# A three-part kernel on one core: the first layer's sums of results spread over four points, and two attention groups re-timed

## The chip, the cores and the metric

The kernel runs on one core of a Trainium2 chip. The metric is the device time of one launch in microseconds (us). Three runs of the kernel before gave 1128.75, 1129.05 and 1133.09 us, median 1129.05.

## The reference

```python
# chunked attention: 4 x 8 heads, 768 positions, 64 wide, chunks of 32 with 16 left, 8 right, 8 memory rows
scores = scale * np.matmul(q_c, k_full.transpose(0, 1, 3, 2))
scores = scores - np.max(scores, axis=-1, keepdims=True)
a = np.exp(scores); a = a / (np.sum(a, axis=-1, keepdims=True) + 1e-09)
out[:, :, c_start:c_end] = np.matmul(a, v_full)
x = attn_out.transpose(0, 2, 1, 3).reshape(3072, 512)
# layer 1
h = x @ w_in; r = np.maximum(h, 0.0); x = (r * r) @ w_out          # 512 -> 2048 -> 512
# layer 2
h = x @ w_in2; sp = log1p(exp(h)); out = (h * np.tanh(sp)) @ w_out2
```

## The kernel before

The 3072 tokens are three groups of 1024. A layer takes eight steps for each group, and each step handles 256 of the 2048 inner columns. So steps 0 to 7, 8 to 15 and 16 to 23 are the first layer of groups 1, 2 and 3, and steps 24 to 47 the second layer. In a step the kernel multiplies tokens by the first weights in seven block products instead of eight (a Strassen-like scheme, so sums and differences of blocks are needed as operands), applies the activation, and in the next step multiplies by the second weights in eight "units" that are added up in the tiles y0 and y1 (512 columns of 4 x 128 rows each). Each operand is held as a rounded part and a rest, so a product is six matmuls of 128x512.

A step of the first layer is thus 15 stretches of six matmuls. Between them are 15 "points", numbered 0 to 14, where the order written by hand puts everything else. Below, 9.3 is point 3 of step 9. `at(s, i, work)` (L634) plans work for a point, `rest()` (L677) is called once at each point: it first issues the stores that `later()` collected (`flush`, L129), then the loads of weights, then the planned work. The points of a first-layer step follow the products P1, P6, P5, then units 0 and 1, then P2, P7, then units 2, 3, 4, then P4, P3, then units 5, 6, 7. Each engine runs its instructions in the order in which they are written, and all DMAs go out in order on one queue, SP, whose instruction waits until the buffer that it writes or reads is ready; what is behind it waits too.

What is planned beside the products:

- Attention. The tokens' 12 blocks of 256 (p = 0 to 11) are attended four to a group. Group 1's (p 0 to 3) comes before step 0; group 2's (p 4 to 7) is planned in steps 0 to 6, group 3's (p 8 to 11) in steps 9 to 14. `plan_attention` (L638) gives each block's works at fixed distances: scores S at 0, softmax at 1 and 2, exponentials and the next block's k load at 3, normalization and the v load at 5, transposes T at 12, the next q load at 13, values V at 16, copy and block differences (on POOL) at 17 and 18, the store of the result at 22. `start, first, period` (L882) say where the blocks begin and how far apart they are.
- The input of a group, written by those stores, is loaded in the group's last step before (`load_x`, at points 0 to 6 of steps 7, 15 and 23), then rounded on ACT and its rest taken on DVE (`split_x`, L275 and L277).
- The weights are unpacked (DVE L154 to L158) and split (`plan_w`): rounding R, r on ACT, rests L, l on DVE, stores to DRAM (`w_d<-hi`, `w_d<-val`).
- The first layer's result of a group. `sums_y` (L615), called at the end of steps 8, 16 and 24, stores three blocks of y0 and y1 (b11 and b21 are the halves of y0, b12 and b22 those of y1) and computes four differences T1 = b12-b11, T2 = b22-T1, T3 = b22-b12, T4 = b21-T2 on DVE (L628) into fresh tiles, which are stored too.

Buffers have names ("tags"), and a new tile of a tag waits for the users of the old one. The tags of this change: y0 and y1; at0 (k of groups 2 and 3, two x loads, T1 and T2 before); at1 (v and the result `stage` of groups 2 and 3, two x loads, T3 and T4 before); xt0 to xt2 (q, p, transposed p, x loads, a weight's rounded half).

After P6 the DVE adds u1 to the bank of P6 (u2, L744), and P7 reuses that bank; u3 (L763) does the same after P7, c21 is L771, c12 L776. L549 adds a unit to y and frees its bank; in a group's first step ACT copies instead (L547).

Of the kernel before, what the change touches and what calls it, by code (L numbers as in the profile page):

```python
# [53 lines left out]
def tile_chunk_attention_moe_moe2(  # L54
# [470 lines left out]
    def unit(s, t, d, rest):  # L525

        layer, sb, j = where(s)
        ps = bank(3 + units[0] % (3 if sb < NSB - 1 else 5))
        units[0] += 1
        w = w2_t[s].rearrange("p c (b f) -> p c b f", b=4)  # L530

        blk = lambda f: (2 + f, f)[d // 2]
        order = [(f, a, 0) for f in range(2) for a in range(2)] + [(f, 0, 1) for f in range(2)]
        for i, (f, a, c) in enumerate(order):
            nc.tensor.matmul(  # L535
                out=ps,
                lhsT=w[:, a, blk(f), d % 2 * 128:d % 2 * 128 + 128],
                rhs=g_t[s, (f, t)][:, c, :],
                start=i == 0,
                stop=i == len(order) - 1,  # L540
            )
        rest()
        if j == 0 and d == 0:
            y_t[sb, t] = pool.tile([128, KD, NB], FP32, tag=f"y{t}", name="y")
        y = y_t[sb, t][:, d]
        if j == 0:
            nc.scalar.copy(out=y, in_=ps)  # L547
        else:
            nc.vector.tensor_tensor(out=y, in0=ps, in1=y, op=ALU.add)  # L549
# [62 lines left out]
        store_y(sb, i, t, m)  # L612
        flush()

    def sums_y(sb):  # L615
        d = xt_d[1][sb]
        y0, y1 = y_t[sb, 0], y_t[sb, 1]
        b11, b21, b12, b22 = (i.rearrange("p k s -> p (k s)") for i in (y0[:, 0:2], y0[:, 2:4], y1[:, 0:2], y1[:, 2:4]))
        nc.sync.dma_start(out=d[:, B11], in_=b11)
        nc.sync.dma_start(out=d[:, B21], in_=b21)  # L620
        nc.sync.dma_start(out=d[:, B22], in_=b22)
        if sb < NSB - 1:
            both = [pool.tile([128, 2, 2 * NB], FP32, tag=f"at{n}", name="ty") for n in range(2)]
            t = [both[n // 2][:, n % 2] for n in range(4)]
        else:
            t = [pool.tile([128, 2 * NB], FP32, tag=("xt0", "xt1", "xt2", "at1")[n], name="ty") for n in range(4)]
        for n, (t1, t2) in enumerate(((b12, b11), (b22, t[0]), (b22, b12), (b21, t[1]))):
            nc.vector.tensor_tensor(out=t[n], in0=t1, in1=t2, op=ALU.subtract)  # L628
            later(d[:, T1 + n], t[n])


    beside = {}

# [4 lines left out]
    def plan_attention(s, i, p):  # L638

        for n, work in {  # L640
# [1 line left out]
            1: lambda: softmax(p, 0),  # L642
            2: lambda: softmax(p, 1),
            3: lambda: (exps(p, 0), exps(p, 1), load_k(p + 1) if (p + 1) % PSB else None),
            5: lambda: (normalize(p), load_v(p) if p > PSB else None),
            12: lambda: transpose_p(p),
            13: lambda: (copy_pt(p), load_q(p + 1) if (p + 1) % PSB else None),
            16: lambda: values(p),
# [2 lines left out]
            22: lambda: store_x(p),  # L651
        }.items():
            at(s, i + n, work)

    def plan_w(s, i, e, order, round_, split, val):

# [15 lines left out]
    def step(s):  # L672
# [113 lines left out]
            for w in beside.pop((s, i), []):  # L786
                w()
        flush()
        if prev and where(s - 1)[0] == 0 and where(s - 1)[2] == NQ - 1:
            sums_y(where(s - 1)[1])  # L790

    with tc.manual_schedule():
        nc.scalar.preload_act_table_set("natural_log_exp_and_others")
# [74 lines left out]
        seconds = [e for e in order_w if e[0]]  # L868
        for n, e in enumerate(seconds):
            if n < NQ - 1:  # L870
                plan_w(NQ + n, 0, e, "Aa|D|d|RS|s|L||||r|l", lambda e, i: round_w2(e, i, "xt2"), split_w2, "val")
            else:
                n -= NQ - 1
                hi = (["xt0", "xt1"], ["xt2", "at1"])[n % 2]
# [4 lines left out]

        for sb in range(NSB - 1):  # L880
            p = PSB * (sb + 1)
            start, first, period = ((0, 4, 25), (NQ + 1, 8, 19))[sb]  # L882
            at(start, 0, lambda p=p: load_q(p))
            if sb:
                at(start, 0, lambda p=p: load_k(p))
            for n in range(PSB):
                plan_attention(start, first + period * n, p + n)

        for sb in range(1, 2 * NSB):
            s = sb * NQ - 1  # L890
# [80 lines left out]
```

## Time and profile before

| | us |
|---|---|
| median of three runs | 1129.05 |
| the profiled execution, its own time | 1126.08 |
| its span (first to last instruction) | 1124.2 |
| TensorE (PE) busy in the span | 1061.5 |
| VectorE (DVE) busy | 898.6 |
| ScalarE (ACT) busy | 561.6 |
| GpSimd (POOL) busy | 430.5 |

The span is the time from the first to the last instruction of the profiled execution; its own time is 1.9 us longer. A time in a row is counted from the span's start. L480 is a product with the first weights, L535 a unit, L346 and L354 scores, L416 values. The step that begins at a given time can be told from the L480 row of 18 matmuls (P1, P6, P5) that opens it: steps 7, 8, 9 and 10 begin at 239.34, 264.87, 288.82 and 324.82 us.

How to read the rows further down: in "busy time by stretch" stand the stretch, its length, then busy us and (number of instructions) of PE, PE's weight loads, DVE, ACT and POOL, then the granted clock of PE as a share of its full 2.4 GHz, the busy share of the DMA engines and GB/s. In a "timeline" stand start, length, engine, line, operation, out<-in, shapes and count of instructions merged, and in brackets the idle time before them and what ended it. SPq is an instruction that issues a DMA; its length is the time that issuing took.

### The profile page before, as it was taken

To read this page: it belongs to the slowest core of one execution; us is meant where nothing else is said; L and a number is where in the kernel's file an instruction comes from. 1 tells how busy PE (TensorE), PEld (TensorE's weight loads), DVE (VectorE), ACT (ScalarE), POOL (GpSimd) and SP (SyncE) were. 2 spreads that over 40 slices of the span, in tenths; PEclk is the share of its full clock that TensorE was granted. 3 is DMA by queue.
4 is the path that set the end of the run, shared out by engine and by line. 5 is a ranking of instruction groups with operands and counts; after the bars stand their busy time and mean duration, and the time that the engine had idled before them with its cause. 6 is when DMAs were issued, how large, how long until landed. Compare 5 with 4: busy or idle time off the path is not lost.

```text
span 1124.2 us, 19766 instructions
## 1 busy us (share of the span) xinstructions
PE 1061.5 (94%) x7478; PEld 872.3 (78%) x7478; DVE 898.6 (80%) x1170; ACT 561.6 (50%) x879; POOL 430.5 (38%) x327
## 2 busy tenths in 40 slices
PE   5779999897799999999999999999999999999997
PEld 5758787785677887888888878888878888778885
DVE  5686889969756766578999767988888888978888
ACT  2458555546544554647656555443354444444331
POOL 1215233232223333223322244546454554545552
PEclk9998999999989999999999999999999999999999
DMA  9556867777989898969999968989979889797441
GB/s 354 216 186 269 308 228 275 259 265 268 369 316 319 306 333 298 336 237 381 374 345 328 361 225 292 316 312 324 401 247 319 308 307 371 272 315 227 158 155 75
DMA packets 192125, 324.94 MB, mean 289 GB/s; under 512 B 13344, under 2 KB 151072, under 8 KB 188192
## 3 DMA queue, kind: packets, MB, share of 16 engines
q1 hardware_dynamic: 192032, 323.69, 80.9%
q8 instruction: 60, 0.98, 0.3%
q14 instruction: 33, 0.27, 0.1%
HBM read 231.62 MB, written 92.01 MB: 288 GB/s over the span
## 4 chain that ended last, share of the span: by engine, by line
PE 65%; DVE 14%; DMA 6%; issue 4%; ACT 3%; POOL 1%; SPq 0%; DVEq 0%; ACTq 0%; POOLq 0%
PE banks L480 29%; PE banks L535 16%; PE banks L570 15%; DVE m L558 3%; PE banks L416 1%; PE banks L346 1%; DVE r L521 1%; DMA w_d<-hi 1%; DMA w2s<-w_d 1%; DVE y L549 1%; DMA w1s<-w_d 1%; DVE ty L628 1%; DVE val L157 1%; DVE val L158 1%; DVE val L154 1%
## 5 line engine op out<-in xcount | busy, mean ns | idle before, releaser
L480 PE MATMUL banks<-x,w1s 128*128 128x512 f32 x2016 | 502.2, 396 | 19.1 <-DVE u L763 7.3
L494 POOL TENSOR_TENSOR g<-r,g 128x512 fp32r<-128x512 f32 x206 | 289.6, 1412 | 523.1 <-ACT g L493 434.6
L480 PEld LDWEIGHTS banks<-x,w1s 128*128 128x128 f32 x2016 | 382.3, 191 | 104.4 <-DVE u L763 9.0
L535 PE MATMUL banks<-g,w2s 128*128 128x512 f32 x1152 | 279.7, 394 | 6.9 <-DVE y L549 6.7
L535 PEld LDWEIGHTS banks<-g,w2s 128*128 128x128 f32 x1152 | 216.7, 190 | 55.7 <-DVE y L549 8.4
L570 PE MATMUL banks<-g,w2s 128*128 128x512 f32 x966 | 239.0, 390 | 1.2 <-DVE m L558 0.6
L570 PEld LDWEIGHTS banks<-g,w2s 128*128 128x128 f32 x966 | 180.6, 188 | 41.9 <-DVE m L558 2.3
L558 DVE TENSOR_TENSOR m<-banks,m 128x1024 f32<-128x1024 f32 x144 | 173.3, 1218 | 30.5 <-PE banks L570 27.5
L493 ACT CAST g<-r 128x512 fp32r<-128x512 f32 x206 | 127.0, 621 | 31.0 <-DVE r L521 23.7
L549 DVE TENSOR_TENSOR y<-banks,y 128x512 f32<-128x512 f32 x168 | 111.4, 682 | 25.7 <-PE banks L535 25.4
L494 POOL TENSOR_TENSOR g<-more,g 128x512 fp32r<-128x512 f32 x55 | 81.8, 1492 | 77.8 <-ACT g L493 63.2
L499 ACT ACTIVATE r<-r 128x512 f32<-128x512 f32 x72 | 45.4, 631 | 69.5 <-DVE r L771 46.1
L503 ACT ACTIVATE r<-r 128x512 f32<-128x512 f32 x48 | 30.3, 632 | 75.8 <-DVE r L765 38.4
L213 ACT CAST hi<-val 128x1024 fp32r<-128x1024 f32 (+1 forms) x32 | 30.4, 951 | 71.4 <-DVE val L158 42.3
L500 ACT ACTIVATE r<-r 128x512 f32<-128x512 f32 x96 | 60.7, 633 | 3.1
L154 DVE TENSOR_SCALAR val<-val 128x512 f32<-128x512 f32 x64 | 36.7, 573 | 24.4 <-ACT val L147 24.4
L346 PE MATMUL banks<-k,q 64*32 64x64 f32 x1536 | 39.4, 255 | 16.8 <-DMA k<-k_dram 10.1
L346 PEld LDWEIGHTS banks<-k,q 64*32 64x32 f32 x1536 | 33.4, 125 | 21.5 <-issue 18.2
L158 DVE SCALAR_TENSOR_TENSOR val<-raw,val 128x512 uint32<-128x512 uint32 x64 | 47.3, 738 | 2.2
L735 ACT COPY u<-banks 128x512 f32<-128x512 f32 x48 | 27.9, 581 | 41.1 <-PE banks L480 41.0
L386 POOL TENSOR_TENSOR p<-p,sum 128x512 f32<-128x512 f32 x22 | 25.6, 1186 | 57.8 <-DVE sum L383 23.3
L416 PE MATMUL banks<-pt,v 64*64 64x32 f32 x1536 | 35.1, 249 | 11.3 <-ACT pt L404 9.8
(72 smaller groups left out, 991.4 us busy)
## 6 DMA issues: line engine op xcount, KB each, us to landing
w1s<-w_d SPq DMA_DIRECT2D x280, 256.0 KB, 5.5
w2s<-w_d SPq DMA_DIRECT2D x229, 256.0 KB, 5.4
raw<-w_dram SPq DMA_DIRECT2D x64, 512.0 KB, 5.1
w_d<-w1s SPq DMA_DIRECT2D x8, 1792.0 KB, 7.1
x<-xs_d SPq DMA_DIRECT2D x14, 1024.0 KB, 10.7
k<-k_dram SPq DMA_DIRECT2D x24, 512.0 KB, 7.3
v<-v_dram SPq DMA_DIRECT2D x24, 512.0 KB, 8.7
xt<-xt_d SPq DMA_DIRECT2D x21, 512.0 KB, 7.3
```

The source lines that it names most:

```text
L154: nc.vector.tensor_scalar(out=val, in0=val, scalar1=LIMIT, scalar2=-LIMIT * NEGATIVE, op0=ALU.min, op1=ALU.max)
L158: nc.vector.scalar_tensor_tensor(out=vb, in0=low, scalar=29, in1=vb, op0=ALU.logical_shift_right, op1=ALU.bitwise_or)
L346: nc.tensor.matmul(out=s4[32 * c:32 * c + 32, j, hp, :], lhsT=q_t[p][r0:r0 + 64, j, hp, 32 * c:32 * c + 32], rhs=k_t[p][r0:r0 + 64, j, hp, ...
L416: nc.tensor.matmul(out=x_ps[par][64 * h2:64 * h2 + 64, o:o + 32], lhsT=v_t[p][j][r0:r0 + 64, h2, a, c, :], rhs=pt_t[p][r0:r0 + 64, h2, j, ...
L480: nc.tensor.matmul(out=ps, lhsT=w[:, a, f:f + 128], rhs=x[:, xi, c, kk, :], start=start and i == 0, stop=stop and i == len(order) - 1, ski ...
L493: nc.scalar.copy(out=g[:, 0], in_=r)
L494: nc.gpsimd.tensor_tensor(out=g[:, 1], in0=r, in1=g[:, 0].bitcast(FP32), op=ALU.subtract)
L500: nc.scalar.activation(out=r, in_=r, func=ACTF.Square)
L535: nc.tensor.matmul(out=ps, lhsT=w[:, a, blk(f), d % 2 * 128:d % 2 * 128 + 128], rhs=g_t[s, (f, t)][:, c, :], start=i == 0, stop=i == len(o ...
L549: nc.vector.tensor_tensor(out=y, in0=ps, in1=y, op=ALU.add)
L558: engine.tensor_tensor(out=to, in0=in0, in1=in1, op=ALU.add)
L570: nc.tensor.matmul(out=bank(first + d), lhsT=w[:, a, 128 * d:128 * d + 128], rhs=g[:, c, :], start=i == 0, stop=i == 2)
```

## The change

The four differences are planned at points instead of after a step: T1 at point 13 of the group's last unit step (8.13, 16.13, 24.13), T2, T4 and T3 at points 0, 1 and 3 of the next. T1 and T2 go into one tile of tag at1; T4 and T3 overwrite b21 and b12 in y0 and y1, so the tag at0 is not used any more, and the next group keeps the same y tiles. The stores of b11 and b21 are planned at points 5 and 9. Group 3's attention begins at 8.10 (before 9.8) with 20 points from block to block (before 19); its k is loaded at 8.1 (before 9.0). Group 2's has 24 points from block to block (before 25). The v load comes 8 points after the scores instead of 5. In steps 8 to 14 the second half of a weight is rounded and split a point later.

```diff
@@ unit
-            y_t[sb, t] = pool.tile([128, KD, NB], FP32, tag=f"y{t}", name="y")
+            y_t[sb, t] = y_t[sb - 1, t] if sb else pool.tile([128, KD, NB], FP32, tag=f"y{t}", name="y")
@@
-    def sums_y(sb):
-        d = xt_d[1][sb]
...
-        nc.sync.dma_start(out=d[:, B11], in_=b11)
-        nc.sync.dma_start(out=d[:, B21], in_=b21)
-        nc.sync.dma_start(out=d[:, B22], in_=b22)
-        if sb < NSB - 1:
-            both = [pool.tile([128, 2, 2 * NB], FP32, tag=f"at{n}", name="ty") for n in range(2)]
...
-        for n, (t1, t2) in enumerate(((b12, b11), (b22, t[0]), (b22, b12), (b21, t[1]))):
-            nc.vector.tensor_tensor(out=t[n], in0=t1, in1=t2, op=ALU.subtract)
-            later(d[:, T1 + n], t[n])
@@ plan_attention
-            5: lambda: (normalize(p), load_v(p) if p > PSB else None),
+            5: lambda: normalize(p),
+            8: lambda: load_v(p) if p > PSB else None,
@@
+    def plan_sums(sb):
...
+        def minus(n, to, in0, in1):
+            nc.vector.tensor_tensor(out=to, in0=in0, in1=in1, op=ALU.subtract)
+            later(d[:, n], to)
+        def first():
+            b11, _, b12, _ = blocks()
+            t["both"] = pool.tile([128, 2, 2 * NB], FP32, tag="at1", name="ty")
+            minus(T1, t["both"][:, 0], b12, b11)
+        def second():
+            b22 = blocks()[3]
+            later(d[:, B22], b22)
+            minus(T2, t["both"][:, 1], b22, t["both"][:, 0])
+        def fourth():
+            b21 = blocks()[1]
+            minus(T4, b21, b21, t["both"][:, 1])
+        def third():
+            _, _, b12, b22 = blocks()
+            minus(T3, b12, b22, b12)
+        s = (sb + 1) * NQ
+        at(s, 5, lambda: later(d[:, B11], blocks()[0]))
+        at(s, 9, lambda: later(d[:, B21], blocks()[1]))
+        at(s, 13, first)
+        at(s + 1, 0, second)
+        at(s + 1, 1, fourth)
+        at(s + 1, 3, third)
@@ step
-        if prev and where(s - 1)[0] == 0 and where(s - 1)[2] == NQ - 1:
-            sums_y(where(s - 1)[1])
@@
-                plan_w(NQ + n, 0, e, "Aa|D|d|RS|s|L||||r|l", lambda e, i: round_w2(e, i, "xt2"), split_w2, "val")
+                plan_w(NQ + n, 0, e, "Aa|D|d|RS|s|L|||||r|l", lambda e, i: round_w2(e, i, "xt2"), split_w2, "val")
@@
-            start, first, period = ((0, 4, 25), (NQ + 1, 8, 19))[sb]
+            start, first, period = ((0, 4, 24), (NQ, 10, 20))[sb]
             at(start, 0, lambda p=p: load_q(p))
             if sb:
-                at(start, 0, lambda p=p: load_k(p))
+                at(start, 1, lambda p=p: load_k(p))
             for n in range(PSB):
                 plan_attention(start, first + period * n, p + n)
+        for sb in range(NSB):
+            plan_sums(sb)
```

On DVE, from the end of step 8 into step 9, the kernel before has c12, the last three units, the four differences in a row, one weight half unpacked and then u2:

```order
L776 TENSOR_TENSOR r<-banks,u_2918 128x512
L549 TENSOR_TENSOR y<-banks,y 128x512 x3
L628 TENSOR_TENSOR ty<-y 128x1024
L628 TENSOR_TENSOR ty<-y,ty 128x1024
L628 TENSOR_TENSOR ty<-y 128x1024
L628 TENSOR_TENSOR ty<-y,ty 128x1024
L154 TENSOR_SCALAR val<-val 128x512
L157 TENSOR_SCALAR val<-val 128x512
L158 SCALAR_TENSOR_TENSOR val<-raw,val 128x512
L744 TENSOR_TENSOR u_3107<-banks,u_3093 128x512
```

The same place after the change, from unit 5 on (L651 is a difference, L380 to L383 the normalization of p 8, L769 is u2):

```order
L549 TENSOR_TENSOR y<-banks,y 128x512
L651 TENSOR_TENSOR ty<-y 128x1024
L549 TENSOR_TENSOR y<-banks,y 128x512 x2
L380 TENSOR_REDUCE sum<-p 128x8 x2
L382 TENSOR_SCALAR sum<-sum 128x16
L383 RECIPROCAL sum<-sum 128x16
L651 TENSOR_TENSOR ty<-y,ty 128x1024
L154 TENSOR_SCALAR val<-val 128x512
L157 TENSOR_SCALAR val<-val 128x512
L158 SCALAR_TENSOR_TENSOR val<-raw,val 128x512
L651 TENSOR_TENSOR y<-y,ty 128x1024
L769 TENSOR_TENSOR u_3194<-banks,u_3177 128x512
```

T1 stands among the last units, T2 and T4 are still ahead of u2, and T3 has moved behind it; p 8's normalization is new in this place.

On the SP queue the kernel before issues, at the end of step 8 and the begin of step 9, the stores of the result and only behind them group 3's first q and k:

```order
L619 DMA xt_d<-y 128x1024
L620 DMA xt_d<-y 128x1024
L621 DMA xt_d<-y 128x1024
L131 DMA xt_d<-ty 128x1024 x4
L247 DMA w1s<-w_d 128x2x256
L313 DMA q<-q_dram 128x1024
L318 DMA k<-k_dram 128x1024 x2
L247 DMA w2s<-w_d 128x2x256
```

After the change the queue has, from 8.13 to 9.4 (the first row is p 9's k; p 8's has gone out at 8.1):

```order
L318 DMA k<-k_dram 128x1024 x2
L131 DMA xt_d<-ty 128x1024
L247 DMA w1s<-w_d 128x2x256
L131 DMA xt_d<-y 128x1024
L131 DMA xt_d<-ty 128x1024
L247 DMA w2s<-w_d 128x2x256
L131 DMA raw<-w_dram 128x1024
L131 DMA xt_d<-y 128x1024
L247 DMA w1s<-w_d 128x2x256
L131 DMA raw<-w_dram 128x1024
L331 DMA v<-v_dram 128x1024 x2
L131 DMA xt_d<-y 128x1024
```

The loads of p 8's v, which take the tile of T1 and T2, stand ahead of the store of T3, the last row.

On the same queue the last block of group 2 is stored at the end of step 6. The kernel before:

```order
L131 DMA raw<-w_dram 128x1024 x4
L131 DMA w_d<-w1s 128x3584
L442 DMA xt_d<-stage 128x1792
L131 DMA w_d<-w2s 128x2048
L247 DMA w1s<-w_d 128x2x256
L261 DMA xt<-xt_d 128x4x256 x2
```

The kernel after:

```order
L131 DMA raw<-w_dram 128x1024 x3
L442 DMA xt_d<-stage 128x1792
L131 DMA raw<-w_dram 128x1024
L131 DMA w_d<-w1s 128x3584
L131 DMA w_d<-w2s 128x2048
L247 DMA w1s<-w_d 128x2x256
L261 DMA xt<-xt_d 128x4x256 x2
```

The store has moved past a raw load and a weight store, away from the loads of x that read what it writes.

## Rows read from the trace of the kernel before

**Rows 1.** Busy time by stretch, steps 7 to 10 and step 17.

```profile
239.34:264.87 25.53, 21.59 (x91) 16.59 (x90) 16.38 (x23) 12.61 (x19) 5.58 (x4) 1.00 1.03 377
264.87:288.82 23.95, 21.50 (x92) 16.54 (x90) 19.47 (x30) 13.64 (x20) 5.80 (x4) 1.00 0.72 236
288.82:324.82 36.00, 28.06 (x235) 22.41 (x234) 23.41 (x34) 17.76 (x30) 6.79 (x5) 0.86 1.02 379
324.82:354.23 29.41, 28.23 (x371) 23.36 (x370) 17.49 (x28) 16.63 (x28) 11.38 (x11) 0.94 0.84 289
494.12:514.52 20.40, 20.40 (x91) 16.89 (x90) 16.92 (x27) 12.04 (x21) 3.75 (x4) 1.00 0.94 329
```

**Rows 2.** Timeline of PE, steps 8 and 9.

```profile
270.25 2.98 PE L535 MATMUL banks<-g,w2s 128*128 128x512 f32 x12 [1.13 <-DVE y L549]
...
276.21 1.64 PE L480 MATMUL banks<-x,w1s 128*128 128x512 f32 x6 [1.16 <-DVE u L744]
...
300.26 1.67 PE L480 MATMUL banks<-x,w1s 128*128 128x512 f32 x6 [3.12 <-DVE u L744]
...
307.35 0.65 PE L346 MATMUL banks<-k,q 64*32 64x64 f32 x32 [2.56 <-DMA k<-k_dram]
308.55 0.37 PE L346 MATMUL banks<-k,q 64*32 64x64 f32 x11 [0.54 <-DMA k<-k_dram]
...
313.83 0.31 PE L346 MATMUL banks<-k,q 64*32 64x64 f32 x1 [1.72 <-issue]
```

**Rows 3.** Timeline of SP, begin of step 9.

```profile
293.59 4.83 SPq L131 DMA_DIRECT2D xt_d<-ty  x4
...
300.50 0.88 SPq L318 DMA_DIRECT2D k<-k_dram  x2
```

**Rows 4.** Busy time by stretch, two stretches of lower granted clock.

```profile
308.84:319.06 10.22, 8.50 (x119) 7.11 (x108) 3.64 (x5) 1.63 (x2) 0.20 (x1) 0.50 1.04 380
349.80:353.20 3.40, 3.40 (x10) 2.71 (x9) 1.12 (x2) 1.06 (x2) 1.57 (x2) 0.50 0.72 236
```

**Rows 5.** Timeline of PE, step 7.

```profile
254.51 3.02 PE L480 MATMUL banks<-x,w1s 128*128 128x512 f32 x12 [1.40 <-DVE u L763]
259.04 1.65 PE L535 MATMUL banks<-g,w2s 128*128 128x512 f32 x6 [1.51 <-DVE y L549]
261.65 3.39 PE L535 MATMUL banks<-g,w2s 128*128 128x512 f32 x12 [0.96 <-DVE y L549]
```

**Rows 6.** Timeline of ACT, step 7.

```profile
251.54 1.05 ACT L275 CAST x<-xt 128x1024 fp32r<-128x1024 f32 x1 [8.54 <-DMA xt<-xt_d]
```

**Rows 7.** Chain that ended last, end of step 6: start, us, what.

```profile
237.51 0.71 POOL stage L438
...
238.24 8.18 DMA xt_d<-stage
```

**Rows 8.** Timeline of DVE, begin of step 9.

```profile
291.38 2.19 DVE L628 TENSOR_TENSOR ty<-y 128x1024 f32<-128x1024 f32 x1
...
295.73 1.21 DVE L628 TENSOR_TENSOR ty<-y 128x1024 f32<-128x1024 f32 x1
...
299.52 0.68 DVE L744 TENSOR_TENSOR u<-banks,u 128x512 f32<-128x512 f32 x1
```

**Rows 9.** Groups of instructions of the whole span: busy us, mean ns | idle before.

```profile
L369 DVE TENSOR_REDUCE mx<-banks 128x8 f32<-128x512 f32 x24 | 16.4, 684 | 28.2 <-PE banks L346 17.7 <-PE banks L354 10.6
L380 DVE TENSOR_REDUCE sum<-p 128x8 f32<-128x512 f32 x24 | 15.5, 679 | 1.6 <-ACT p L376 1.4
```

**Rows 10.** Timeline of PE, step 13.

```profile
412.62 0.81 PE L346 MATMUL banks<-k,q 64*32 64x64 f32 x43 [0.99 <-ACT stage L428]
```

**Rows 11.** DMA issues by line: KB each, median us from issue to landing.

```profile
v<-v_dram SPq DMA_DIRECT2D x24, 512.0 KB, 8.7
...
xt_d<-ty SPq DMA_DIRECT2D x12, 512.0 KB, 3.1
```

**Rows 12.** Timeline of POOL, begin of step 9.

```profile
291.19 1.29 POOL L494 TENSOR_TENSOR g<-r,g 128x512 fp32r<-128x512 f32 x1 [5.18 <-ACT g L493]
```

More of the change, by code (lines that the diff above doesn't have):

```diff
@@ L613, in last_unit @@
         flush()
-    def sums_y(sb):
-        d = xt_d[1][sb]
-        y0, y1 = y_t[sb, 0], y_t[sb, 1]
-        b11, b21, b12, b22 = (i.rearrange("p k s -> p (k s)") for i in (y0[:, 0:2], y0[:, 2:4], y1[:, 0:2], y1[:, 2:4]))
-        nc.sync.dma_start(out=d[:, B11], in_=b11)
-        nc.sync.dma_start(out=d[:, B21], in_=b21)
-        nc.sync.dma_start(out=d[:, B22], in_=b22)
-        if sb < NSB - 1:
-            both = [pool.tile([128, 2, 2 * NB], FP32, tag=f"at{n}", name="ty") for n in range(2)]
-            t = [both[n // 2][:, n % 2] for n in range(4)]
-        else:
-            t = [pool.tile([128, 2 * NB], FP32, tag=("xt0", "xt1", "xt2", "at1")[n], name="ty") for n in range(4)]
-        for n, (t1, t2) in enumerate(((b12, b11), (b22, t[0]), (b22, b12), (b21, t[1]))):
-            nc.vector.tensor_tensor(out=t[n], in0=t1, in1=t2, op=ALU.subtract)
-            later(d[:, T1 + n], t[n])
     beside = {}
@@ L653, in plan_attention, with blocks @@
             at(s, i + n, work)
+    def plan_sums(sb):
+        d = xt_d[1][sb]
+        t = {}
+        def blocks():
+            y0, y1 = y_t[sb, 0], y_t[sb, 1]
+            return [i.rearrange("p k s -> p (k s)") for i in (y0[:, 0:2], y0[:, 2:4], y1[:, 0:2], y1[:, 2:4])]
+        def minus(n, to, in0, in1):
[22 more added lines that the diff above has]
+        at(s + 1, 3, third)
     def plan_w(s, i, e, order, round_, split, val):
```

## The prediction

> **What bounds the kernel now.** The times by stretch come first: PE is busy through nearly every step, so a step's length beside that of an undisturbed one says what may be had. Step 17 has neither attention nor idle PE: 90 matmuls in 20.40 us, or 1.36 us for each of its 15 points. Steps 7 to 10 take 25.53, 23.95, 36.00 and 29.41 us [rows 1]; step 9 stands out, with 7.94 us of idle PE (36.00 less 28.06) and a granted clock of 0.86. The timeline of PE says what ends the idle times there. In step 9 PE waits 3.12 us for u2 on DVE, then 2.56 and 0.54 us for k of p 8, then 1.72 us for nothing that the profile shows ("issue") [rows 2]. The wait for u2: the four differences stand in a row ahead of it on DVE, from 291.38 on, and u2 starts at 299.52 [rows 8]. The wait for k: the loads leave SP at 300.50, behind the four stores of the differences, whose issue takes from 293.59 to 298.42 because each waits for its difference [rows 3]; k also takes the tile of T1 and T2. Behind that, 10.22 us stand at a granted clock of 0.50, which is 1.2 GHz, after a stretch of idle PE and score products; a second one, of 3.40 us, follows p 9's scores [rows 4]. Step 7 has another cause: ACT stands 8.54 us until the first x block has landed [rows 6], because its source, the last store of group 2, left at 238.24 as soon as POOL had the differences and took 8.18 us [rows 7]. DVE is late behind ACT, and PE waits 1.40, 1.51 and 0.96 us in step 7 [rows 5], then 1.13 and 1.16 us in step 8 [rows 2].
>
> **The change, term by term.** Attention's own work on PE is the same in all (a block's products move from one step to another), so I count waits and clock only, against the profiled execution's 1126.08 us.
>
> k of p 8. It leaves at 8.1, some 10 points before the scores at 8.10, about 14 us at 1.36. Before, the same loads needed 8 us (300.50 to the end of the wait at 308.55 [rows 2, 3]). At 8.1 its tile at0 must be free of the fourth x block of step 7, whose rest comes on DVE at 7.12; a delay there of a few us is covered. So the 2.56 and 0.54 us go: -3.10. If k is late after all, 0. The "issue" wait of 1.72 us sits inside the scores and no engine ends it: it moves with them, 0.
>
> Clock. In the 10.22 us at 0.50 PE is busy 8.50 us [rows 4]; at full speed that work would take 4.25 us, so it costs at most 4.25. Score products are small and gain less than dense ones: I take -3.5 with the wait ahead of it gone, between 0 and -4.25. The 3.40 us after p 9's scores cost at most 1.70; their place moves from 10.12 to 10.0, where the same drop may come or not: -0.85, the middle.
>
> Step 7. With a period of 24, p 7's values come three points earlier (6.2 for 6.5), so its differences on POOL and its store should be ready about 3 x 1.36 = 4.1 us earlier; and on SP the store has moved past a raw load and a weight store. It would land about 242.3 for 246.4, and ACT's wait of 8.54 us falls to about 4.4, nearer to the point (7.4, about 245 to 246) where ACT would not have done the rounding sooner anyway. The three waits of PE in step 7 are the tail of that delay and sum to 3.87, less than the 4.1 gained: -3.87, between 0 (if POOL or SP is late for another reason) and that. Of step 8's 1.13 + 1.16 = 2.29 the same backlog is a part; I take -1.3, between +1.7 and -2.29: step 8 gets p 8's softmax as new work on DVE, two reductions of 0.68 us [rows 9] and two subtractions of the same size, plus T1 of 1.21 to 2.19 [rows 8]. That makes 19.47 + 2.7 + 1.7 = 23.9 us of DVE for a PE step of 20.40 plus the scores, near 22.4; the excess of 1.5 to 1.7 is what is late next if it is not taken up by step 7's slack (DVE 16.38 of 25.53 us [rows 1]).
>
> u2 in step 9. Ahead of it T1 is gone to step 8 and T3 has moved behind: two of four differences, 3.3 us of the 6.6 between 291.38 and 298.0. New ahead of it are p 8's two sums of normalization, 2 x 0.68 [rows 9], and a small rest, together 1.8. So of 3.12 some 1.6 stay: -1.5, between 0 and -3.12.
>
> The bank for scores. In step 13 p 11's scores wait 0.99 us for ACT to have copied p 10's values out of the bank [rows 10]. Period 20 gives the copy a point more: -0.5, between 0 and -0.99.
>
> What is added. T4 and T3 lie in y0 and y1, and group 2's first units are copied there by ACT (9.7 on for b21, 9.9 on for b12), which must wait until the stores have landed. T2's store goes at 9.1, and p 8's v, which takes the tile of T1 and T2, is loaded at 9.3: SP waits there for the landing, and T3's store stands behind v. A store of a difference takes 3.1 us in the median, of all 12 [rows 11]; beside heavy traffic the store of a block took 8.18 [rows 7]. v then has until 9.11, eight points or 10.9 us, and needs 8.7 [rows 11]: with 3.1 it is in time, with 8.18 late by about 3. Behind ACT's wait at 9.9 stand the rounding of a weight half and the gates of c21 and c12, whose results are needed four points into step 10, so a few us are covered. I take +1.5 for both, nearer to the quiet end because two points lie between T2 and v, and keep 0 to +6. In steps 17 and 25 there is no v behind the differences; 0.
>
> In steps 1 to 6 the two points' shift leaves each block's work in its step; 0, with a bound of 3.5 both ways, one stretch at the lower clock more or less [rows 4].
>
> Sum: -3.10 - 3.5 - 0.85 - 3.87 - 1.3 - 1.5 - 0.5 + 1.5 = -13.1, so 1113.0 for an execution like the profiled one. The runs' median, 1129.05, is 3.0 above that execution's time; the forecast for a median is 1129.05 - 13.1 = 1116.
>
> One rule weighs against the change. T1 took 2.19 us beside POOL, which worked from 291.19 on [rows 12], and T3 of the same shape 1.21 without it [rows 8]. The Trainium skill ("SBUF", Who interferes with whom) says that a DVE instruction with two SBUF inputs contends with a GpSimd instruction that reads SBUF, and that the one that comes second waits for the whole of the first; the two rows agree. At 9.0 POOL gets p 8's normalization in addition, beside T2 and T4; by the rule both take 2.19, 1 us more in all than the mean used above, and the sum is -12.1.
>
> **The rivals.**
>
> DVE is the bound of step 8. For it: 19.47 us of 23.95 busy already, and about 4.4 added. Against it: DVE is idle for 9.15 of step 7's 25.53 us, and without ACT's wait it can start step 8 without a backlog. Then step 8 keeps its 2.29 (the 1.3 taken is lost) and grows by 1.7, and u2 keeps its 3.12 (1.5 lost): 4.5 less than forecast, 1120.5.
>
> The clock takes it back. For it: both stretches at 0.50 follow score products with a wait among them [rows 2, 4], and every scores, transposes and values of eight blocks changes place. Against it: group 3's four blocks have twelve such places, and two of them show a drop. Three new stretches of the price of the larger one, 3.5 each, are 10.5 us: 1126, no change.
>
> The change does not do what it says, k still late: 3.10 + 3.5 come back, 1123.
>
> Slower: the differences in place hold up the queue. SP goes in order: T2 waits for DVE, v for T2's landing, T3's store for v's issue, group 2's copies of b12 for T3. If DVE is 4.5 us late (the first rival) and each transfer takes 8 to 9 us, v lands 4.5 + 8.18 + 8.7 = 21.4 us after T2's point and is due after some 11 points, 15 us, so that PE stands 6.4 us at 9.11 and gets the lower clock (3.5); T3's store follows v and lands as late as v, five points after ACT should have copied b12, so that the bank is missing to unit 7: up to 6.8. With the DVE's 4.5 that is 6.4 + 3.5 + 6.8 + 4.5 = 21.2, 8 more than the gain: 1137 at its worst; from 13.1 on it decides against the change. Against it: 3.1 us for such a store in the median.
>
> **How the numbers follow.** The forecast with its own range, 1109 to 1119, gets 0.58; DVE as the bound of step 8, 0.20; clock, 0.11; k late, 0.04; slower, 0.07. All terms at their full size would be 3.10 + 4.25 + 1.70 + 3.87 + 2.29 + 3.12 + 0.99 = 19.3, and with 3.5 from steps 1 to 6 22.8: 1106, the low end. The high end is the clock's, 1126. A measurement of this kernel can tell about 0.5%, 5.6 us, from no change. Faster by more, under 1123.4: the forecast, the first rival and half of the third, 0.80; within 0.5%: the clock and the rest of k late, 0.13; slower: 0.07.
>
> **What would show it.** Right: in step 9 no wait for k in the timeline of PE, a wait before P7 of about 1.6 us, a granted clock of 1.00 in steps 8 and 9; in step 7 ACT's wait for x at about half and PE's three waits gone; step 9 at about 25 us. Wrong: a wait before p 8's values for v, ACT waiting for a store of y in steps 9, 17 or 25, step 8 above 25 us, or new stretches at 0.50 in steps 1 to 14.

## The result, and the profile after

The changed kernel takes 1115.71 us, the median of four runs (1112.70 to 1119.03); the kernel before took 1128.9 beside it. The ratio is 0.9877 with an interval of 0.9839 to 0.9915, so it is faster, by 13 us. The profiled execution took 1115.43 us (span 1113.6; before 1126.08 and 1124.2). The two profiles thus differ by 10.6 us, less than the medians do: single executions of one kernel lie some us apart, and so each reading below of a few tenths on a whole step is one execution's.

Where the 10.6 us are, by places in the program (from the first matmul of the first step named to the first behind the last):

| place | before | after | difference | forecast there |
|---|---|---|---|---|
| up to step 1 | 78.76 | 77.53 | -1.23 | 0 |
| steps 1 to 6 | 160.58 | 158.01 | -2.57 | 0 |
| step 7 | 25.53 | 24.48 | -1.05 | -3.87 |
| steps 8 to 14 | 188.06 | 182.74 | -5.32 | -9.25 |
| steps 15 to 23 | 184.44 | 184.55 | +0.11 | 0 |
| steps 24 and 25 | 41.15 | 39.44 | -1.71 | 0 |
| behind step 25 | 445.68 | 446.85 | +1.17 | 0 |

The total came out as forecast, the places did not: the steps that the prediction worked on (7 to 14) gave 6.4 of the 13.1 us. The first and the last row are scatter: up to step 1 the thirteen kernels profiled (these two and the eleven of the experiments) take 77.5 to 78.9 us, behind step 25 from 445.7 to 448.4, whatever was changed.

Busy time by stretch of the kernel after: steps 7 to 10 (the first four rows answer to [rows 1]), steps 8 to 14, and steps 24 and 25:

```profile
235.54:260.02 24.48, 21.59 (x92) 16.58 (x90) 16.47 (x23) 12.70 (x19) 5.60 (x4) 1.00 1.02 378
260.02:286.96 26.94, 24.45 (x236) 19.03 (x234) 22.45 (x35) 16.18 (x25) 7.03 (x5) 1.00 0.89 311
286.96:315.06 28.10, 25.23 (x227) 20.55 (x226) 19.16 (x29) 14.11 (x25) 7.82 (x5) 0.94 1.02 379
315.06:341.99 26.93, 24.57 (x243) 20.10 (x242) 17.95 (x32) 15.37 (x26) 10.23 (x11) 1.00 0.87 319
260.02:442.76 182.74, 171.83 (x1736) 139.86 (x1734) 129.59 (x208) 95.24 (x155) 61.28 (x52) 0.98 0.89 316
627.31:666.75 39.44, 39.44 (x175) 32.67 (x174) 28.77 (x33) 23.57 (x34) 17.50 (x12) 1.00 0.83 273
```

The same for the kernel before, steps 8 to 14, and steps 24 and 25:

```profile
264.87:452.93 188.06, 174.25 (x1735) 142.25 (x1734) 131.12 (x211) 98.97 (x160) 60.92 (x53) 0.96 0.89 313
637.37:678.52 41.15, 40.03 (x176) 32.51 (x174) 28.25 (x33) 23.33 (x34) 17.17 (x12) 1.00 0.75 260
```

Single steps can't be set side by side, because score products have moved (step 8 has x236 matmuls for x92, step 9 x227 for x235); the seven together can, with x1736 and x1735. Idle PE in them fell from 13.81 to 10.91 us (length less the first number behind it), busy PE by 2.42. With the same number of products it is the clock that makes busy time differ: at 0.50 stood 10.22 + 3.40 us before [rows 4], and 3.41 + 3.41 after:

```profile
297.70:301.11 3.41, 2.96 (x7) 2.39 (x8) 3.31 (x7) 1.46 (x3) 0.00 (x0) 0.50 0.98 331
383.03:386.44 3.41, 3.41 (x32) 2.77 (x25) 1.23 (x2) 2.04 (x5) 1.31 (x2) 0.50 0.97 312
```

The timeline of PE after, steps 7 to 10, waits only (start, length, instruction, wait ahead of it and what ended it), answers to [rows 2, 5]:

```profile
249.65 3.02 PE L480 MATMUL banks<-x,w1s 128*128 128x512 f32 x12 [0.35 <-DVE u L788]
254.18 1.66 PE L535 MATMUL banks<-g,w2s 128*128 128x512 f32 x6 [1.52 <-DVE y L549]
256.79 3.39 PE L535 MATMUL banks<-g,w2s 128*128 128x512 f32 x12 [0.95 <-DVE y L549]
...
265.39 3.00 PE L535 MATMUL banks<-g,w2s 128*128 128x512 f32 x12 [1.13 <-DVE y L549]
...
271.41 1.64 PE L480 MATMUL banks<-x,w1s 128*128 128x512 f32 x6 [1.21 <-DVE u L769]
...
298.15 2.93 PE L480 MATMUL banks<-x,w1s 128*128 128x512 f32 x6 [2.87 <-DVE u L769]
...
318.16 0.33 PE L346 MATMUL banks<-k,q 64*32 64x64 f32 x8 [1.58 <-ACT stage L428]
```

The two waits for k and the "issue" wait of step 9 are gone; the waits of step 8 stand as they were; u2's is 2.87 for 3.12; and p 9's scores in step 10 have a new one of 1.58.

### The profile page after: what moved, and what is told of

It reads as the page before. It is cut to its first block, busy times and chain, and to the rows that moved or that the text cites. A ratio compares the mean times of both kernels' runs of the same rounds, so it can differ in the third digit from the quotient of the medians.

```text
span 1113.6 us, 19772 instructions
## 1 busy us (share of the span) xinstructions
PE 1056.0 (95%) x7478; PEld 867.1 (78%) x7478; DVE 903.5 (81%) x1170; ACT 561.1 (50%) x879; POOL 432.8 (39%) x327
## 4 chain that ended last, share of the span: by engine, by line
PE 59%; DVE 9%; DMA 3%; issue 2%; ACT 1%; SPq 0%; DVEq 0%; ACTq 0%
PE banks L480 28%; PE banks L570 17%; PE banks L535 13%; DVE m L558 3%; DMA w_d<-hi 2%; DMA w_d<-val 1%; DVE r L521 1%; DVE more L521 0%; DVE y L549 0%; DVE u L769 0%; DVE val L220 0%; PE banks L346 0%; PE banks L416 0%; DVE val L157 0%; DVE val L154 0%
## 5 line engine op out<-in xcount | busy, mean ns | idle before, releaser
L213 ACT CAST hi<-val 128x1024 fp32r<-128x1024 f32 (+1 forms) x32 | 30.4, 950 | 76.0 <-DVE val L158 43.5
L154 DVE TENSOR_SCALAR val<-val 128x512 f32<-128x512 f32 x64 | 41.1, 642 | 29.8 <-ACT val L147 29.8
L220 DVE TENSOR_TENSOR val<-val,hi 128x1024 f32<-128x1024 f32 (+1 forms) x32 | 36.3, 1136 | 19.3 <-ACT hi L213 19.0
L158 DVE SCALAR_TENSOR_TENSOR val<-raw,val 128x512 uint32<-128x512 uint32 x64 | 48.1, 751 | 2.2
L386 POOL TENSOR_TENSOR p<-p,sum 128x512 f32<-128x512 f32 x22 | 27.1, 1251 | 52.6 <-DVE sum L383 25.5
L147 ACT ACTIVATE val<-raw 128x512 f32<-128x512 f32 x64 | 40.2, 664 | 11.9 <-DMA w_d<-val 11.8
```

Source lines behind the costliest of these rows:

```text
L147: nc.scalar.activation(out=val, in_=high.bitcast(FP32), func=ACTF.Prelu, scale=REBIAS, alpha=NEGATIVE)
L154: nc.vector.tensor_scalar(out=val, in0=val, scalar1=LIMIT, scalar2=-LIMIT * NEGATIVE, op0=ALU.min, op1=ALU.max)
L158: nc.vector.scalar_tensor_tensor(out=vb, in0=low, scalar=29, in1=vb, op0=ALU.logical_shift_right, op1=ALU.bitwise_or)
```

## Experiments

The theory: the time comes from k behind the differences and from the lower clock that followed that wait, so the four points alone should bring most of it. The rivals: the shorter period of group 2, the early start of group 3, or the places of v and of the weight half carry it. Ratios are to the kernel before, with 95% intervals; lengths are of one profiled execution each.

**The differences at four points, alone.** The kernel before, with the shared tiles of y and `plan_sums` as in the change, all else old:

```diff
-        if prev and where(s - 1)[0] == 0 and where(s - 1)[2] == NQ - 1:
-            sums_y(where(s - 1)[1])
+        for sb in range(NSB):
+            plan_sums(sb)
```

> Theory A (k's loads stood behind the differences' stores and took their tile): the differences at four points alone take k out of that queue, so the wait for k in step 9 (3.10 us) goes with the lower clock behind it, step 25 keeps the gain of the spread differences, 1120 to 1123 beside 1129. Rival B (the gain is the 13 points by which group 3's attention begins earlier): with the blocks in their old places little is gained, 1126 to 1128, and step 9 stays above 32 us.

Measured: 1124.27 us, 0.9963 (0.9944 to 0.9983). No wait for k is left, yet steps 8 to 14 take 190.11 us, 2 more than before. The timeline of PE in this kernel, steps 9, 10 and 13, shows what stands there instead:

```profile
297.85 1.66 PE L480 MATMUL banks<-x,w1s 128*128 128x512 f32 x6 [1.33 <-ACT u L759]
...
309.20 0.31 PE L346 MATMUL banks<-k,q 64*32 64x64 f32 x1 [1.96 <-issue]
...
342.18 0.32 PE L346 MATMUL banks<-k,q 64*32 64x64 f32 x8 [1.33 <-ACT r L499]
347.80 0.80 PE L346 MATMUL banks<-k,q 64*32 64x64 f32 x18 [3.18 <-issue]
...
414.01 0.81 PE L346 MATMUL banks<-k,q 64*32 64x64 f32 x43 [2.35 <-ACT stage L428]
```

And its stretches of lower clock there, by busy time:

```profile
346.68:353.50 6.82, 5.70 (x30) 4.47 (x30) 2.67 (x4) 1.85 (x3) 2.23 (x3) 0.50 0.79 283
414.95:421.77 6.82, 6.82 (x104) 5.88 (x96) 3.23 (x5) 1.25 (x2) 4.31 (x5) 0.50 0.92 309
309.13:312.54 3.41, 3.34 (x10) 2.59 (x11) 0.69 (x1) 0.63 (x2) 0.99 (x1) 0.50 1.04 397
```

Step 9 falls from 36.00 to 29.72 us; steps 10 and 13 give it back (34.40 and 31.43 us, for 29.41 and 26.57 before). So the wait was rightly named, but all that the four points change, steps 24 and 25 included, is worth about 4 us (0.0037 of 1127): 17.05 us stand at 0.50 in steps 8 to 14 for 13.62 before, in other places, behind other waits in or ahead of scores. The theory holds for the wait and falls for the time (1120 to 1123).

**Group 3's early start undone.** The changed kernel with the old start, first point and period of group 3:

```diff
-            start, first, period = ((0, 4, 24), (NQ, 10, 20))[sb]
+            start, first, period = ((0, 4, 24), (NQ + 1, 8, 19))[sb]
```

> The kernel after with group 3's blocks back at 9.8, period 19. Theory A: no wait for k either, within 3 us of the kernel after (1113 to 1119). Rival B: it loses most of the gain, 1122 to 1127.

Measured: 1115.49 us, 0.9893 (0.9866 to 0.9920), against 0.9877 of the change: the early start isn't what brings the gain. Step 9 then waits in its scores, 2.83 us of "issue", but step 10 has no wait for the stage copy. The thirteen profiles of this document agree on that trade. In steps 8 to 14 the seven kernels with the old start, the one before among them, have "issue" waits of PE of 2.7 to 5.1 us in sum and wait 0.6 to 2.4 us for the stage copy in step 13; the six with the early start have no "issue" wait there, and five of them wait 0.8 to 2.7 us for the stage copy in step 10.

**Group 2's period undone, and alone.** The changed kernel with period 25, and the kernel before with period 24:

```diff
-            start, first, period = ((0, 4, 24), (NQ, 10, 20))[sb]
+            start, first, period = ((0, 4, 25), (NQ, 10, 20))[sb]
```

> The kernel after with group 2's period back at 25. Forecast's step: p 7's store leaves later, step 7 takes 1 us more (24.5 to 25.5) and steps 1 to 6 some 2.5 us more: 1118 to 1120. Rival: the period decides nothing that can be measured, 1114 to 1117, and steps 1 to 6 differ by where the lower clock falls.

```diff
-            start, first, period = ((0, 4, 25), (NQ + 1, 8, 19))[sb]
+            start, first, period = ((0, 4, 24), (NQ + 1, 8, 19))[sb]
```

> The kernel before with group 2's period 24 and nothing else. Theory A after the first four runs: the period is worth 3 to 5 us in steps 1 to 7, because the stretches at granted clock 0.50 near 83 and 138 us shorten (together 13.7 us before) and p 7's store leaves earlier; 1123 to 1126 with steps 1 to 6 at 158 us for 160.6. Rival: these stretches fall by chance; 1127 to 1130 and 160 to 161 us.

Measured: 1118.28 us, 0.9906 (0.9876 to 0.9936) without it; 1127.06, 0.9985 (0.9971 to 0.9998) with nothing else. The first is 3.3 us above the change (0.0029 of 1127), with intervals that overlap; the second is 1.7 us below the kernel before, barely clear of noise, and its time lies in the range of the rival, though its steps 1 to 6 fit the theory. So the period is worth some 2 to 3 us, not surely. Steps 1 to 6 by busy time, of the kernel without it and of the change beside it:

```profile
78.23:238.79 160.56, 150.51 (x1501) 123.69 (x1500) 137.19 (x216) 96.15 (x155) 59.65 (x49) 0.96 0.71 257
```

```profile
77.53:235.54 158.01, 146.26 (x1502) 119.45 (x1500) 138.66 (x216) 95.64 (x155) 59.61 (x49) 0.99 0.72 263
```

And of the kernel with the period alone:

```profile
77.77:236.63 158.86, 149.47 (x1502) 122.15 (x1500) 137.88 (x215) 96.37 (x156) 59.81 (x49) 0.97 0.72 263
```

All four profiled kernels with period 25 take 160.25 to 160.76 us for steps 1 to 6; of the nine with 24, eight take 155.3 to 159.4 and one 160.5. But these times go with the time at 0.50 in these steps. All four kernels with period 25 have 13.65 us there (two stretches of 6.83, from 82.98 and 137.60 on in the first row); so have three of the nine with 24, and they take 158.9 to 160.5 us. The one with 10.24 takes 158.9, the three with 3.41 take 157.4 to 158.2, the two with none 155.3 and 156.7. Between the first two rows PE is busy for 4.25 us less with period 24 and idle for 1.70 us more. So the gain in steps 1 to 6, forecast at nothing, is in these profiles that of the clock; that the shorter period makes its low stretches rarer is likely, not shown; at the same 13.65 us the three with period 24 lie 0.1 to 1.6 us below the mean of the four with 25. In step 7 the period shows in every profile: 25.5 to 26.3 us with period 25, 24.5 to 24.9 with 24 (without the early loads further down).

The kernel with the period alone shows one thing more. Its k loads still stand behind the four stores (they leave SP at 297.05), and yet PE does not wait for k: a stretch at 0.50 from 296.13 on slows the products ahead (twelve of a unit take 4.51 us, before 3.02), and the scores begin only at 303.98. The timeline of PE in step 9 has this wait instead:

```profile
310.15 0.26 PE L346 MATMUL banks<-k,q 64*32 64x64 f32 x1 [3.61 <-issue]
```

Step 9 takes 36.47 us there, for 36.00 before. The waits and the lower clock stand in for each other, and one that is gone need not shorten the step.

**Both undone.** The changed kernel with both old rows of start, first point and period. It differs from the differences alone by v's place (8 points behind the scores for 5), the second half of a weight one point later, and k's loads one point later:

```diff
-            start, first, period = ((0, 4, 24), (NQ, 10, 20))[sb]
+            start, first, period = ((0, 4, 25), (NQ + 1, 8, 19))[sb]
```

> The kernel after with both groups' attention back in its old places (period 25; from 9.8, period 19): the differences at four points, the v load at 8, the later second half of a weight and k at 9.1 are left. Theory A': v and the later half carry what the differences alone lacked, so about 3 to 4 us behind the kernel with group 3 undone alone: 1117 to 1120 beside 1128. Rival: they carry nothing and the gain needs the periods; 1122 to 1125 as the differences alone.

Measured: 1118.36 us, 0.9914 (0.9888 to 0.9940), where the differences alone had 0.9963 (0.9944 to 0.9983). The intervals don't overlap: these three small moves are worth some 5 us (0.0049 of 1128, give or take 0.0033), no less than the differences alone. Steps 8 to 14 take 178.84 us for 190.11, but a single execution says little there: the two kernels with group 3 undone that differ in step 7 alone (without and with the early x loads further down) take 178.80 and 187.73 us for them.

The ratios make a chain: 0.9963 with the differences alone, 0.9914 with the three small moves, 0.9893 with the period, 0.9877 with the early start. Only its first two steps are clear of noise.

**Which of the three.** The weight half back one point in the changed kernel, and v back at 5 in the kernel with group 3 undone:

```diff
-                plan_w(NQ + n, 0, e, "Aa|D|d|RS|s|L|||||r|l", lambda e, i: round_w2(e, i, "xt2"), split_w2, "val")
+                plan_w(NQ + n, 0, e, "Aa|D|d|RS|s|L||||r|l", lambda e, i: round_w2(e, i, "xt2"), split_w2, "val")
```

> The kernel after with the second half of a weight rounded at 9 and split at 10 again. Theory A: little, 0 to +2 us, ACT waits for the first half's store one point earlier in each of steps 8 to 14 and the copies of units 2 to 4 in step 9 stand behind it. Rival D (this part carries what the differences alone lack beside the kernel with group 3 undone, 8 us): +4 to +8, steps 8 to 14 at 187 to 190 for 182.7.

```diff
-            5: lambda: normalize(p),
-            8: lambda: load_v(p) if p > PSB else None,
+            5: lambda: (normalize(p), load_v(p) if p > PSB else None),
```

> Group 3 undone and the v load back at 5 as well. Theory A': at 5 the v load stands on SP behind the store of the block before, and the weight loads and rounded halves behind it; 2 to 5 us more than with group 3 undone alone (1117 to 1120 beside 1128), in steps 10 to 14. Rival: v's place is free, 1114 to 1117.

Measured: 1118.81 us, 0.9910 (0.9889 to 0.9931), for the weight half; 1116.91, 0.9912 (0.9890 to 0.9935), for v, against 0.9893 (0.9866 to 0.9920) of the same kernel with v at 8. Neither is told apart from its own base. With v at 5 and period 24 the kernel still beats the differences alone by 0.0051, of which the period has 0.0015, so the later half and k's point seem to carry the larger part; that is a difference of differences, not a measurement. What the half's place does is seen in ACT's timeline when it is put back:

```profile
312.01 1.05 ACT L213 CAST hi<-val 128x1024 fp32r<-128x1024 f32 x1 [3.21 <-DMA w_d<-hi]
...
318.65 1.06 ACT L428 COPY stage<-banks 128x512 f32<-128x512 f32 x2
```

The rounding (L213) needs the tile that the half before is still being stored from. One point earlier ACT stands 3.21 us for it, in the changed kernel 1.69; the stage copy behind it ends later, and PE waits 2.68 us for it at p 9's scores instead of 1.58. v's share and the half's stay open.

**The four differences in a row, in place.** The changed kernel with all four at the old place:

```diff
-        at(s, 13, first)
-        at(s + 1, 0, second)
-        at(s + 1, 1, fourth)
-        at(s + 1, 3, third)
+        at(s + 1, 0, first, second, third, fourth)
```

> The kernel after with its four differences in a row at point 0 of steps 9, 17 and 25, still in place. Theory A: k is not touched; only the wait for u2 grows by the two differences that come back ahead of it, 2.4 to 3.3 us in step 9 (from 2.87 to 5 to 6) and step 25 loses its 1.7: 1119 to 1121. Rival C: the spreading is worth nothing since DVE has the same work in steps 8 and 9 anyway: 1114 to 1117.

Measured: 1117.51 us, 0.9908 (0.9882 to 0.9933), between the two forecasts and not told apart from the change. u2 waits 3.19 us, where 5 to 6 were expected; in the changed kernel it is 2.87, and in three others with the same order there 2.14 to 3.17 (early x, period 25, weight half back). With k gone from behind them, the row of differences costs little in step 9. In step 25 the two waits of before return:

```profile
656.25 1.65 PE L480 MATMUL banks<-x,w1s 128*128 128x512 f32 x6 [0.53 <-DVE u L766]
659.85 1.65 PE L570 MATMUL banks<-g,w2s 128*128 128x512 f32 x6 [0.59 <-ACT m L581]
```

Steps 24 and 25 take 41.19 us here, 41.15 before and 41.49 with the period alone; every kernel with the four points takes 39.4 to 39.9. So the 1.7 us of step 25 belong to the four points.

**T4 one point later, behind u2.**

```diff
-        at(s + 1, 1, fourth)
+        at(s + 1, 2, fourth)
```

> The kernel after with T4 one point later (9.2, 17.2, 25.2), behind u2. Theory A: the wait for u2 is DVE's queue ahead of it; it falls by T4's 1.22 us from 2.87 to about 1.65 and the step by as much or a little more through the clock. Rival: something else sets it (unpacking beside POOL's normalization, or ACT), the wait stays above 2.5.

Measured: 1117.32 us, 0.9896 (0.9878 to 0.9914), the same as the change. The timeline of PE in step 9:

```profile
298.48 1.67 PE L480 MATMUL banks<-x,w1s 128*128 128x512 f32 x6 [0.96 <-DVE u L769]
306.49 3.03 PE L480 MATMUL banks<-x,w1s 128*128 128x512 f32 x12 [1.33 <-DVE u L788]
310.23 0.30 PE L416 MATMUL banks<-pt,v 64*64 64x32 f32 x2 [0.71 <-ACT pt L404]
```

u2's wait falls by 1.91, more than T4's own 1.22, as T4 is gone from ahead of it, and 1.33 and 0.71 come up behind: the step takes 27.73 us for 28.10. DVE's backlog is only handed on.

**x of step 7 loaded three points earlier.** In the changed kernel, the first two x blocks' loads are planned at 6.12 and 6.13, behind the store they read, instead of at 7.0 and 7.1:

```diff
-                at(s, o, lambda sb=sb, o=o: load_x(sb, o))
+                at(s, o if sb > 1 or o > 1 else o - 3, lambda sb=sb, o=o: load_x(sb, o))
```

> The kernel after with the first two x loads of step 7 planned three points earlier (6.12, 6.13), so that they leave as soon as the store has landed. Theory A: PE's waits in step 7 (2.82 us) come from the time at which x lands, which is now set by the loads' own 8.7 to 8.8 us beside two weight stores; the first lands 2 to 3 us earlier, the waits fall to under 1.5 us, steps 7 and 8 together from 51.4 to about 49.5. Rival C: the waits are DVE's own work in the order written (rests of x between unpacking and units); arrival changes nothing, 51 to 52.

Measured: 1111.67 us, 0.9847 (0.9830 to 0.9864), the fastest of all, though its interval overlaps the change's. Step 7 takes 21.46 us for 24.48, with one wait of 0.39 left; ACT's wait for x is 4.52 us:

```profile
237.52:258.98 21.46, 20.98 (x92) 16.74 (x90) 16.33 (x23) 12.65 (x18) 5.20 (x4) 1.00 1.04 387
```

```profile
245.49 1.05 ACT L275 CAST x<-xt 128x1024 fp32r<-128x1024 f32 x1 [4.52 <-DMA xt<-xt_d]
```

Step 8's two waits stand as before, 1.13 and 1.20: they don't come from step 7.

**The two best together**, group 3 undone and x early (both edits above):

> Group 3 undone and the first two x loads of step 7 three points earlier. The two gains add if they are independent: 3 us in step 7 and 2 to 4 us in steps 8 to 14, 1108 to 1111 beside 1128, which would be the fastest so far. Rival: steps 8 to 14 take back what step 7 gives, 1112 to 1115.

Measured: 1112.21 us, 0.9864 (0.9831 to 0.9897), no better than x early alone. Step 13 brings back the old wait for the stage copy, 2.32 us, with 10.24 us at 0.50 from 403.85 on. Its profiled execution was its slowest run, 1119.39.

## Why the prediction was right, and where its steps were not

The total is right (1116 forecast, 1115.71 measured), the sign and the wait for k too. That it fits so closely is luck: of its terms some failed, and 4.3 us from steps that it counted at nothing, with 2.6 us by which the medians differ more than the two profiles, filled the gap.

Of its own signs of being right, the wait for k is gone and step 8's clock is 1.00; u2's wait is 2.87 and not 1.6, step 9 has a clock of 0.94 and 28.10 us instead of 25, ACT's wait in step 7 is not halved. Of its signs of being wrong three came: step 8 above 25 us (26.94), ACT waiting for a store of y in step 9, and new stretches at 0.50 (297.70 and 383.03); no product waited for v.

**k of p 8** (-3.10): right. The loads leave at 265.05 and the scores at 278.68 wait for nothing; every kernel with the four points has lost this wait, but for 0.21 to 0.26 us in four of the five where group 3 stands in its old place. The worth of that alone, though, is about 4 us with all that the four points touch, where the prediction had 3.10 and 3.5 for it: waits and lower clock came up elsewhere.

**Clock** (-3.5 and -0.85): too large for its place. In steps 8 to 14 the time at 0.50 fell from 13.62 to 6.82 us, of which at most half is a cost, so at most 3.4 us are won; busy PE fell by 2.42. The granted clock of step 9 isn't 1.00 as forecast, but 0.94; its stretch at 297.70 begins within u2's wait. The other kernels have from 3.4 to 17 us there, so a single profile says little on this term. The granted clock of every run says more: over 50 runs of the kernel before it is 0.977 to 0.988, 0.984 in the mean, over the four of the change 0.982 to 0.994, 0.989 in the mean. An estimate from these means is 9 us less at 0.50 in the whole kernel, worth at most 4.7: at most, then, the clock gave what was forecast, and in the profiles more of it in steps 1 to 6 (13.65 us at 0.50 before, 3.41 after) than in 8 to 14.

**Step 7** (-3.87, measured -1.05): the step that failed is "ACT's wait of 8.54 us falls to about 4.4", since arrival was made to follow the store, and the loads' own time was left as it was. The store did come earlier, and more so than forecast: it left at 229.29 and took 6.2 us, so it had landed 2.3 us before the loads of x left, which stood at their own points. They left 2.29 us behind the begin of step 7, where before it was 7.09, so they gained 4.8 us, where 4.1 were forecast. But they took 8.8 and 8.7 us where before they took 5.1 and 5.9, and the first block landed only 1.1 us earlier in the step. SP's timeline around them, after:

```profile
229.29 0.42 SPq L442 DMA_DIRECT2D xt_d<-stage  x1
...
233.23 0.33 SPq L131 DMA_DIRECT2D w_d<-w1s  x1
...
236.16 0.33 SPq L131 DMA_DIRECT2D w_d<-w2s  x1
...
237.83 2.96 SPq L261 DMA_DIRECT2D xt<-xt_d  x2
```

ACT's wait after, which answers to [rows 6]:

```profile
246.68 1.05 ACT L275 CAST x<-xt 128x1024 fp32r<-128x1024 f32 x1 [7.37 <-DMA xt<-xt_d]
```

The two weight stores (1792 and 1024 KB) go out 4.6 and 1.7 us ahead of these loads; before, the loads waited for their source until 246.43, 9.5 and 6.6 us behind the weight stores. The wait fell by 1.17 us, and PE's three from 3.87 to 2.82. That x's arrival is what the step hangs on is shown by the early loads: they left 2.8 us earlier in the step, ACT's wait fell to 4.52, close to the 4.4 that this term had wanted, and step 7 to 21.46 us, 4.1 below the kernel before. That the weight stores slow the loads is only argued; the early loads, from 236.97 on, took 8.5 and 10.2 us too, the first with one weight store ahead of it. The Trainium skill ("DMA: Bandwidth & Descriptors", Anatomy of one DMA) gives about 2.0 us plus bytes by 436 GB/s, for DMAs issued by way of GpSimd. An estimate by it for a load of 512 KB is 3.2 us. These loads go through SP, and the 8.8 measured in a step whose DMA share is 1.02 is far above it; no run here has such a load by itself.

**Step 8** (-1.3, measured 0): that "the same backlog is a part" of step 8's 2.29 was wrong: 1.13 and 1.21 stand, and with step 7 undisturbed 1.13 and 1.20. All thirteen profiles have the two within 0.1 us. That the order of DVE's work in step 8 itself sets them is argued; no run changed it. The first rival, DVE as the bound there, was not seen either: 26.94 us less 23.95 is 2.99, and the scores of p 8 alone span 2.66 (278.68 to 281.34).

**u2** (-1.5, measured -0.25): that two of four differences are gone from ahead of it was right, what stays ahead was sized wrongly. DVE's timeline before, the rows left out of [rows 8]:

```profile
293.60 2.21 DVE L628 TENSOR_TENSOR ty<-y,ty 128x1024 f32<-128x1024 f32 x1
...
298.00 0.41 DVE L154 TENSOR_SCALAR val<-val 128x512 f32<-128x512 f32 x1
298.45 0.43 DVE L157 TENSOR_SCALAR val<-val 128x512 uint32<-128x512 uint32 x1
298.91 0.69 DVE L158 SCALAR_TENSOR_TENSOR val<-raw,val 128x512 uint32<-128x512 uint32 x1
```

DVE's timeline after, which answers to [rows 8]:

```profile
292.10 1.16 DVE L651 TENSOR_TENSOR ty<-y,ty 128x1024 f32<-128x1024 f32 x1
293.18 1.26 DVE L154 TENSOR_SCALAR val<-val 128x512 f32<-128x512 f32 x1
294.48 1.15 DVE L157 TENSOR_SCALAR val<-val 128x512 uint32<-128x512 uint32 x1
295.67 0.69 DVE L158 SCALAR_TENSOR_TENSOR val<-raw,val 128x512 uint32<-128x512 uint32 x1
296.27 1.22 DVE L651 TENSOR_TENSOR y<-y,ty 128x1024 f32<-128x1024 f32 x1
297.41 0.68 DVE L769 TENSOR_TENSOR u<-banks,u 128x512 f32<-128x512 f32 x1
298.01 0.41 DVE L154 TENSOR_SCALAR val<-val 128x512 f32<-128x512 f32 x1
298.46 0.43 DVE L157 TENSOR_SCALAR val<-val 128x512 uint32<-128x512 uint32 x1
```

And POOL's beside it:

```profile
292.32 3.03 POOL L386 TENSOR_TENSOR p<-p,sum 128x512 f32<-128x512 f32 x2 [1.86 <-ACT val L147]
```

The unpacking ahead of u2 (L154 to L158) stood there before as well and took 1.5 us; now it takes 3.1, since its first two instructions take 1.26 and 1.15 us beside POOL's normalization of p 8, where they took 0.41 and 0.43. That is the term that the prediction left out. T2 and T4 were not slowed, though the prediction weighed the rule for them: T2 came 0.22 us ahead of POOL and took 1.16 us for 2.21, T4 came after POOL had ended (295.35). The Trainium skill ("SBUF — State Buffer", Who interferes with whom) says that `tensor_scalar` too can take the ports that DVE shares with GpSimd, and that whoever comes second waits; the rows agree. Lastly T1 among the units makes DVE 0.9 us later with them (it is done with the third at 290.50, 3.5 us into the step; before at 291.46, 2.6 us).

**Bank for scores** (-0.5): wrong; step 13's 0.99 is gone, but step 10 has 1.58 for the same copy. The wait has moved with the blocks.

**What is added** (+1.5): the chain came as described, its size fits by chance. v landed at 307.84 and 309.09, and its products wait for nothing; T3's store stood behind it and took 8.8 us. ACT, after:

```profile
310.46 0.58 ACT L547 COPY y<-banks 128x512 f32<-128x512 f32 x1 [1.85 <-DMA xt_d<-y]
312.74 1.05 ACT L213 CAST hi<-val 128x1024 fp32r<-128x1024 f32 x1 [1.69 <-DMA w_d<-hi]
...
317.53 1.06 ACT L428 COPY stage<-banks 128x512 f32<-128x512 f32 x2
```

ACT is held 1.85 us by T3's store and 1.69 by a weight's, and its copy of stage stands behind both; PE meets that as the 1.58 before p 9's scores, the same 1.58 as in the term above. It is the slower rival's chain, seen at a small size; the prediction had only the first of the two waits, and looked for it at later products.

**Counted at nothing.** Steps 1 to 6 gave 2.57 us, by the lower clock of which the prediction had said in its bound of 3.5 that it may come or go there. Steps 24 and 25 gave 1.71 (the four points): there the differences in a row had held DVE too, without v or k behind them, and the prediction looked only for what was added.

## What to carry to other kernels

Removing a wait is worth its length only if nothing behind it waits for something else: after the wait for k went, ACT's copies, "issue" waits and the clock took a good part of the forecast gain back, and three small moves of other work were worth as much as what was left. When a source is made ready earlier, price the reader's own transfer again beside what is then on the way, and move its issue as well. A gain of a few us in one profile may be the lower clock's: set kernels side by side at the same time at 0.50. Where a burst of work recurs in a program, price it at every place, not only where its wait is the longest.

## What the runs showed of the hardware

The "issue" waits of PE, where the profile shows nothing to wait for, follow packets of the instruction queue. A packet of 16 KB ended at 312.53 and PE went on at 313.83 [rows 2]; in the changed kernel step 3 has such a wait, which the kernel before has not:

```profile
141.88 1.90 PE L480 MATMUL banks<-x,w1s 128*128 128x512 f32 x7 [2.82 <-issue]
```

with a packet from 139.57 to 140.53. In all 42 such waits of over 0.9 us in the thirteen profiles (up to 3.61 us) PE resumed 1.22 to 1.71 us behind the end of a 16 KB packet, each amid the many small products of attention or, in step 3, shortly behind them (2.7 us here). These take the most instructions for their time: 126 in 2.06 us from 134.29 on, where 12 large products take 2.88. Most packets pass without a wait. That PE waits for its next instructions is thus likely, and no run tested it. The prediction had moved 1.72 us of this kind along with the scores; behind the early start steps 8 to 14 have none, and the 2.82 of step 3 is new.
